# Four edits to a fused attention-and-routing kernel: who loads the first values, who clears the first tiles, how the weight sums are grouped, and the order of one block's products

## The chip, the cores and the metric

The kernel runs on one core of a Trainium2 chip. The metric is the device time of one execution in microseconds. Three runs of the kernel before took 889.56, 890.16 and 890.52 us; their median, 890.16 us, is the time that the change is measured against. The engines are named as in the profile: PE (matmuls) with its weight loads PEld, DVE (VectorE), ACT (ScalarE), POOL (GpSimd) and SP (SyncE, which here only issues DMAs).

## The reference, cut to what matters

```python
# attention: batch 4, heads 4, seq 1088, head_dim 32, r = 8; S1 and S2 arrive as float64
a = einsum('rd,bhsd->bhsr', S1, x); b = einsum('rd,bhsd->bhsr', S2, x)
phi(x) = outer(a, b) per row                      # 64 features
kv  = sum over s of phi(k) v^T ;  z = sum over s of phi(k)
out = phi(q) kv / (phi(q) z + 1e-6)               # -> x: (4352, 128)
# routing: 8 rounds of row and column normalisation of exp(x @ w_gate) -> P (4352 x 8)
# mixture: for each of 8 experts e
h = maximum(x @ w1[e], 0); out += P[:, e:e+1] * (h @ w2[e])   # w1: 128 x 1024, w2: 1024 x 128
```

The sum over `s` in `kv` and `z` runs over all keys of a batch, so the order in which keys lie in a tile is free as long as the values lie in the same order.

## The kernel before, in words

The kernel has three stretches on PE, one after the other without a break.

**Start (0 to about 21 us).** The loads of batch 0 are issued by SP in this order: S1 (L104; S2 goes by ACT's queue), the keys (`load_k`, L171), the first 8 of 34 rows of the queries (L178), the values (`load_v`, L180 to L189: four quarters of 128 KB at L183 and two short tails at L187), the other queries, then the first weights and batch 1. DVE turns S1 and S2 from float64 into float32 (`f64_to_f32`, L34 to L47), transposes them (`st`, L222) and spreads them over the heads (`wd`, L223). `transpose_k` (L266) then transposes the keys into `kT` in two halves (L269) and a rest (L271); `transpose_q` (L264) does the queries. PE multiplies `kT` by `wd` (L280), ACT copies the result to `ab` (L283), DVE forms the products of features `kp` (L295), and PE sums them against the values (L310, 36 matmuls in nine steps of four; the first four steps use the first half of `kp`). `kvz` (L326), the fractions (L369) and the division (L380 to L387) give `xT`, the input of the experts, and the first expert matmuls (L734) follow. POOL clears several tiles at the start (L113 to L165) and forms the repeated projections `wq` (L230, L231) from `st`. In each of these DVE, ACT and PE run in the order written in the code; POOL and SP are ordered by a scheduler. Every DMA uses one of eight completion semaphores in turn, so an issue also waits until the transfer eight issues before it has landed.

**Unweighted blocks (about 21 to 190 us).** Expert 0, and expert 1 for a part of the rows, in blocks of the hidden units (`steps`, L803). For each block PE computes four pieces `h[0..3]` (L734, relu by ACT at L736), DVE forms the sums `t13` (c = 4: `ts[0]` and `ts[1]` together), then `ts[2]` and `ts[3]` (L749), and PE makes seven products (`seven`, L769 to L784, issued by `into` at L796). Two products on different halves of the array run side by side; `p7` runs alone. `LAG` of 8 puts a block's products behind the pieces of the blocks after it, except at the very end, where no blocks follow. When an accumulator is complete, `part_of_seven` copies it out. In between, the rest of attention and the routing rounds are fitted in.

**Weighted stage (from 190 us).** 60 items (group of rows, expert), each in two halves `s = 0` and `s = 1` of eight steps. `firsts` (L1058) makes seven products per half into two PSUM pairs `pa` and `pc` (L1074), ACT copies some of them out (L1154, L1158, L1161), DVE adds them into `h` (L1084) and forms `ts` (L1131, L1134 to L1136). `seconds` (L1196) of the half before is interleaved step by step (L1224). In the first group, experts 1 to 7 come for the first time ("fresh"): their `w1` is loaded raw (L896) and POOL forms four sums of its parts (`sum_first`, L914: forms 4, 5, 6, 7 at L917 to L920), which are also stored for later groups (L923). `aside` (L1099), called after the third product of a half, hands POOL its work: the weighted inputs of the item after next (`weigh`, L1004), their difference (`sum_x` part 0, L1012), and in `s = 0` all four sums of the next fresh item. A `gate` (L1097) is a one-element copy by ACT into the target, which keeps POOL from starting before that point.

Of the kernel before, what the change touches and what calls it, by code (L numbers as in the profile page):

```python
# [10 lines left out]
F32 = mybir.dt.float32  # L11
U32 = mybir.dt.uint32
Act = mybir.ActivationFunctionType
Alu = mybir.AluOpType
# [4 lines left out]
def f64_to_f32(nc, pool, raw, shape):  # L19


    p, n = shape
    low, high = raw[:, 0::2], raw[:, 1::2]

    def u32(name):
        return pool.tile([p, n], U32, name=name)

    def f32(name):
        return pool.tile([p, n], F32, name=name)

    mant, bits, top, expo, rest = (u32(x) for x in ("mant", "bits", "top", "expo", "rest"))
    out, inside, over = f32("s12"), f32("inside"), bits.bitcast(F32)
    shift_right, shift_left = Alu.logical_shift_right, Alu.logical_shift_left
    nc.vector.tensor_scalar(bits, high, 3, 0x3F800000, op0=shift_left, op1=Alu.bitwise_and)  # L34
    nc.vector.tensor_scalar(mant, high, 3, 0x3FFFFFF8, op0=shift_left, op1=Alu.bitwise_and)
    nc.vector.tensor_scalar(rest, low, 0x1FFFFFFF, None, op0=Alu.bitwise_and)

    nc.vector.scalar_tensor_tensor(top, high, 0xC0000000, bits, op0=Alu.bitwise_and, op1=Alu.bitwise_or)
    nc.vector.scalar_tensor_tensor(mant, low, 29, mant, op0=shift_right, op1=Alu.bitwise_or)
    nc.vector.tensor_scalar(expo, high, 20, 0x7FF, op0=shift_right, op1=Alu.bitwise_and)  # L40
    nc.vector.scalar_tensor_tensor(out, rest, 2.0 ** -52, top.bitcast(F32), op0=Alu.mult, op1=Alu.mult)
    nc.vector.scalar_tensor_tensor(mant, high, 0xC0000000, mant, op0=Alu.bitwise_and, op1=Alu.bitwise_or)

    nc.vector.tensor_scalar(over, expo, 1150.5, 3e38, op0=Alu.is_ge, op1=Alu.mult)
    nc.vector.tensor_tensor(out, out, mant.bitcast(F32), op=Alu.add)
    nc.vector.scalar_tensor_tensor(inside, expo, 896.5, over, op0=Alu.is_ge, op1=Alu.add)
    nc.vector.tensor_tensor(out, out, inside, op=Alu.mult)  # L47
    return out


@with_exitstack
def kernel(
# [12 lines left out]
    nc = tc.nc  # L65
    P = nc.NUM_PARTITIONS
    B, H, S, D = q.shape
    R = S1.shape[0]
# [4 lines left out]
    SA = S // 32  # L73
    NT = S // P
# [5 lines left out]
    H2 = DM // 2  # L80

    consts = ctx.enter_context(tc.tile_pool(name="consts", bufs=1))
# [18 lines left out]
    words = mybir.dt.size(S1.dtype) // 4  # L101
# [32 lines left out]
    qT, kT = (wk.tile([P, 4 * W9], F32, name=n, bufs=1) for n in ("qT", "kT"))  # L134
# [14 lines left out]
    kvs = []  # L149
    for i in range(2):  # L150
        kvs.append(consts.tile([P, 2, 2, D + 1], F32, name=f"kvs{i}"))
        nc.gpsimd.memset(kvs[i], 0.0)

    eps = consts.tile([P, 3, H], F32, name="eps")
    nc.gpsimd.memset(eps, 1e-6 / P)

    v_slots = []
    for i in range(2):
        t = wk.tile([P, H + 1, NT + 1, D], F32, name=f"v{i}", bufs=1)
        nc.vector.memset(t[:, H], 1.0)  # L160
        nc.gpsimd.memset(t[H2:P, 0:H, NT], 0.0)
        v_slots.append(t)

    ab = wk.tile([P, 2, NT + 1, H * R], F32, name="ab", bufs=1)
    nc.gpsimd.memset(ab[H2:P, :, NT], 0.0)  # L165

    loaded, pools = {}, []

# [5 lines left out]
    def load_q(b, lo=0, hi=SA):  # L174
# [2 lines left out]
        x = q[b].rearrange("h (s a) d -> (h s) a d", a=SA)  # L177
        nc.sync.dma_start(out=loaded["q", b][:, lo:hi], in_=x[:, lo:hi])  # L178

    def load_v(b):  # L180
        vx, o = v_slots[b % 2], v[b].offset
        for c in range(4):
            nc.sync.dma_start(  # L183
                out=vx[c::4, 0:H, 0:NT, :].rearrange("p h t d -> p h (t d)"),
                in_=AP(tensor=v.tensor, offset=o + NT * D * c, ap=[[SA * D, 32], [S * D, H], [1, NT * D]]))
        for c in range(2):
            nc.sync.dma_start(  # L187
                out=vx[32 * c:32 * (c + 1), 0:H, NT, :],
                in_=AP(tensor=v.tensor, offset=o + (4 * NT + c) * D, ap=[[SA * D, 32], [S * D, H], [1, D]]))  # L189
# [24 lines left out]
    wd = consts.tile([P, 2, H, R], F32, name="wd")  # L214
# [2 lines left out]

    def projections():
        flat = raw.rearrange("p n d -> p (n d)")
        s12 = f64_to_f32(nc, consts, flat, (P, 2 * D)) if words == 2 else flat.bitcast(F32)  # L220
        st = consts.tile([P, 2, 32], F32, name="st")
        nc.vector.transpose(out=st.rearrange("p n r -> p (n r)"), in_=s12)  # L222
        nc.vector.tensor_tensor(wd, st[:, :, 0:R].unsqueeze(2).to_broadcast([P, 2, H, R]),  # L223
                                own.unsqueeze(1).unsqueeze(3).to_broadcast([P, 2, H, R]), op=Alu.mult)
        return st

# [15 lines left out]
    nothing = consts.tile([P, 1], F32, name="nothing")  # L242
# [23 lines left out]
    def transpose_k(b, parts=((0, NT),)):  # L266
        kx = loaded["k", b]
        for lo, hi in parts:
            nc.vector.transpose(out=kT[:, 0:NT * P].rearrange("p (t s c) -> p c t s", c=4, s=32)[:, :, lo:hi],  # L269
                                in_=kx[:, 0:4 * NT, :].rearrange("p (c t) d -> p c t d", c=4)[:, :, lo:hi])  # L270
        nc.vector.transpose(out=kT[:, NT * P:S], in_=kx[:, 4 * NT:SA, :].rearrange("p a d -> p (a d)"))  # L271

# [347 lines left out]
    loaded_w, sums, parts, done = {}, {}, {}, {}  # L620
# [91 lines left out]
    blocks = [(j, q) for j in range(len(items)) for q in range(FO // 2)]  # L712
# [56 lines left out]
    def seven(k):  # L769

        j, q = blocks[k]
        _, w2, ws = loaded_w[j]
        h, ts, _ = hs[k]
        lo, hi = slice(0, H2), slice(H2, DM)
        p1 = (w2[:, 2 * q, lo], h[0], 0, 0)
        p6 = (ws[:, 1, q], ts[2], 0, 1)
        p2 = (w2[:, 2 * q + 1, lo], h[2], 1, 0)
        p4 = (w2[:, 2 * q + 1, hi], ts[3], 1, 1)
        p3 = (ws[:, 3, q], h[3], 2, 0)
        p5 = (ws[:, 0, q], ts[0], 2, 1)  # L780
        p7 = (ws[:, 2, q], ts[1], 3, k % 2)
        if k % 2 == 0:
            return [p1, p6], [p2, p4], [p3, p5], [p7]
        return [p6, p1], [p4, p2], [p5, p3], [p7]  # L784
# [77 lines left out]
    fresh = {*range(len(wgroups[0][2]))}  # L862
    late = []
    forms, form_stores, weights, sources = {}, {}, {}, {}
    FORM = FO * H2 // 2

    PLACE = {f: n for n, f in enumerate((0, 4, 5, 7, 6, 2, 3, 1))}
# [43 lines left out]
            lo, hi = ((0, 2), (2, 3))[part_ - 2]  # L911
            in_turn(i, nc.sync.dma_start(out=ws[:, lo:hi], in_=f[:, 4 + lo:4 + hi]))

    def sum_first(i):  # L914
        g = nc.gpsimd
        w1 = {f: forms[i][0][:, n] for f, n in PLACE.items()}
        g.tensor_tensor(w1[4], w1[1], w1[3], op=Alu.add)  # L917
        g.tensor_tensor(w1[5], w1[4], w1[0], op=Alu.subtract)
        g.tensor_tensor(w1[6], w1[0], w1[1], op=Alu.subtract)
        g.tensor_tensor(w1[7], w1[2], w1[5], op=Alu.subtract)  # L920

    def store_first(i):
        nc.sync.dma_start(out=form_stores[witems[i][1]][0], in_=forms[i][0][:, 0:7])  # L923
# [116 lines left out]
    def weighted():  # L1040
# [12 lines left out]
        def rooms(t):  # L1053
            n = wgroups[witems[todo[t][0]][0]][1]
            base = hb[:, 4096 * (t % 2):4096 * (t % 2 + 1)]
            return [base[:, 2048 * a:2048 * a + 8 * n].rearrange("p (b n) -> p b n", b=4) for a in range(2)]

        def firsts(t):  # L1058

            i, s = todo[t]  # L1060
            g, e = witems[i]
            n = wgroups[g][1]
            a, c = pairs[::-1] if t % 2 and i else pairs
            w1, xf = forms[i][0], sources[i]
            h, ts = rooms(t)
            pa, pc = a[:, :, 0:n], c[:, :, 0:n]
            p1, p5, u2 = (copies[:, t % 2, m, 0:2 * n] for m in range(3))
# [28 lines left out]
            def gate(x, y):  # L1096
                nc.scalar.copy(x, y)  # L1097

            def aside(y):  # L1099


                if s == (i == 0) and i + 2 < len(witems):
                    weigh(i + 2, lambda x: gate(x, y))
                if 0 < i and i + 1 < len(witems) and s == (g > 0):
                    gate(sources[i + 1][:, 4, 0:1], y)
                    sum_x(i + 1, 0)
                if s == 0:
                    if 1 < i + 1 in fresh:
                        gate(forms[i + 1][0][:, PLACE[4], 0:1], y)
                        sum_first(i + 1)  # L1110
                    if 0 < i in fresh:
                        store_first(i)
                if g == 0:
                    pass
                elif chores and (s or not leisure):
                    chores.pop(0)[1]()
                else:
                    for _ in range(2 if g + 2 >= LAST else 1):
                        leave(nc.gpsimd)
# [279 lines left out]
        for t in range(len(todo) + 1):  # L1399
            if t < len(todo):  # L1400
                i, s = todo[t]
# [14 lines left out]
            s = seconds(t - 1) if t else iter(())  # L1416
# [9 lines left out]
    with tc.manual_schedule(engines={engines.DVE, engines.PE, engines.Activation}):  # L1426
        st = projections()
# [124 lines left out]
```

## Time and profile before

| | |
|---|---|
| median of three runs | 890.16 us |
| the profiled execution: its time / its span | 890.32 us / 888.5 us |
| granted PE clock, as a share of full speed | 1.00 |
| DVE, ACT, POOL busy | 765.5, 544.7, 274.9 us |
| mean DMA rate | 202 GB/s |

Times in the profile count from the start of the span, in microseconds. A row of the timeline has start, busy time, engine, line, operation, output and input tiles, shape and count; idle time of the engine before it and its releaser stand in square brackets. SPq rows are DMA issues, and landings come later. The chain of waits lists, in order of time, which work set the end: start, length, engine, tile, line, count. PE rows of fp32 matmuls count two passes per matmul, so x8 is four matmuls.

### The profile page before, as it was taken

The page shows a single profiled execution, that of the slowest core. Times are in us where ns is not written, and L with a number is a line of the kernel's source. Part 1 is how long each engine was busy: PE and PEld are TensorE (multiplying, and loading weights), DVE is VectorE, ACT ScalarE, POOL GpSimd, SP SyncE. Part 2 cuts the span into 40 slices and gives each one's busy share as a digit, 9 for nine tenths or more (in the row PEclk, how much of TensorE's full clock was granted, in tenths as well). Part 3 has the DMA queues.
Part 4 walks back from the last instruction along what each step waited for, and adds up shares of the span by engine and source line. Part 5 has one row for each costly group of instructions (what it writes and reads, how often), then busy time and mean ns, then how long its engine had stood idle before and what let it go on. Part 6 is the DMA issues. An engine that isn't in the chain of part 4 may idle for free.

```text
span 888.5 us, 36437 instructions
## 1 busy us (share of the span) xinstructions
PE 881.3 (99%) x15308; PEld 651.0 (73%) x15308; DVE 765.5 (86%) x1339; ACT 544.7 (61%) x1086; POOL 274.9 (31%) x316
## 2 busy tenths in 40 slices
PE   8999999999999999999999999999999999999998
PEld 5788656867666777677777777777877887897886
DVE  8689689978898888888888888888899899889996
ACT  3455557646656666666666666666666666666664
POOL 3121125455552223323222322332232233333311
PEclk9999999999999999999999999999999999999999
DMA  7989399887786866477567667655774874774861
GB/s 231 294 268 276 83 219 250 135 243 229 226 256 180 236 204 197 132 220 214 160 174 214 197 170 210 197 170 162 236 232 130 265 236 135 226 245 130 249 198 31
DMA packets 146419, 179.10 MB, mean 202 GB/s; under 512 B 55984, under 2 KB 93568, under 8 KB 145872
## 3 DMA queue, kind: packets, MB, share of 16 engines
q1 hardware_dynamic: 138624, 166.67, 64.6%
q0 software_dynamic: 6528, 9.95, 5.6%
q8 instruction: 121, 1.98, 0.9%
q14 instruction: 42, 0.34, 0.1%
q10 hardware_dynamic: 1104, 0.15, 0.1%
HBM read 134.22 MB, written 25.99 MB: 180 GB/s over the span
## 4 chain that ended last, share of the span: by engine, by line
PE 97%; DVE 2%; DMA 0%; ACT 0%; issue 0%; DVEq 0%; ACTq 0%
PE pair L1074 39%; PE s L1224 38%; PE a L734 9%; PE s L796 7%; PE a L310 1%; PE a L439 1%; DVE kT L269 0%; PE a L280 0%; PE s L349 0%; DVE hb L749 0%; PE s L1240 0%; DMA raw<-in_S_dram 0%; DVE hb L1084 0%; PE a L473 0%; PE a L403 0%
## 5 line engine op out<-in xcount | busy, mean ns | idle before, releaser
L1074 PE MATMUL pair<-xf,w1x 64*64 64x256 f32 (+1 forms) x6736 | 500.1, 366 | 0.2
L1074 PEld LDWEIGHTS pair<-xf,w1x 64*64 64x64 f32 x6736 | 258.7, 133 | 92.0 <-DVE hb L1084 6.3
L1084 DVE TENSOR_TENSOR hb<-pair,copies 128x512 f32<-128x512 f32 (+1 forms) x354 | 233.7, 662 | 63.7 <-PE pair L1074 25.7
L1224 PE MATMUL s<-hb,w 64*64 64x256 f32 (+1 forms) x3824 | 285.1, 365 | 0.0
L1224 PE MATMUL s<-hb,ws 64*64 64x256 f32 (+1 forms) x2848 | 212.6, 365 | 0.0
L1087 ACT ACTIVATE hb<-hb 128x512 f32<-128x512 f32 (+1 forms) x238 | 144.4, 608 | 101.7 <-DVE hb L1084 96.3
L1224 PEld LDWEIGHTS s<-hb,w 64*64 64x64 f32 x3824 | 149.8, 133 | 47.9
L1004 POOL TENSOR_TENSOR xf<-xT,pb 128x512 f32<-128x512 f32 (+1 forms) x60 | 73.9, 1231 | 254.6 <-ACT xf L1097 198.6
L1012 POOL TENSOR_TENSOR xf<-xf 128x512 f32<-128x512 f32 (+1 forms) x59 | 72.9, 1235 | 216.7 <-ACT xf L1097 105.1
L1224 PEld LDWEIGHTS s<-hb,ws 64*64 64x64 f32 x2848 | 111.5, 133 | 35.9 <-issue 0.4
L734 PE MATMUL a<-xT,w 128*64 128x416 f32 (+3 forms) x512 | 122.5, 465 | 0.0
L1087 ACT ACTIVATE hb<-pair 128x512 f32<-128x512 f32 (+1 forms) x126 | 72.5, 576 | 44.3 <-PE pair L1074 44.1
L736 ACT ACTIVATE hb<-a 128x416 f32<-128x416 f32 (+3 forms) x128 | 59.5, 468 | 63.6 <-PE a L734 57.2
L1131 DVE SCALAR_TENSOR_TENSOR hb<-hb 128x512 f32<-128x512 f32 (+1 forms) x118 | 80.6, 683 | 15.9 <-ACT hb L1087 3.4
L1161 ACT COPY copies<-pair 128x512 f32<-128x512 f32 (+1 forms) x118 | 66.5, 563 | 30.8 <-PE pair L1074 30.8
L1158 ACT COPY copies<-pair 128x512 f32<-128x512 f32 (+1 forms) x118 | 66.5, 563 | 29.7 <-PE pair L1074 29.7
L1154 ACT COPY copies<-pair 128x512 f32<-128x512 f32 (+1 forms) x118 | 66.6, 564 | 26.4 <-PE pair L1074 26.4
L1134 DVE TENSOR_TENSOR hb<-hb 128x512 f32<-128x512 f32 (+1 forms) x118 | 79.4, 673 | 2.9
L1136 DVE TENSOR_TENSOR hb<-hb 128x512 f32<-128x512 f32 (+1 forms) x118 | 81.2, 688 | 0.0
L1135 DVE SCALAR_TENSOR_TENSOR hb<-hb 128x512 f32<-128x512 f32 (+1 forms) x118 | 80.6, 683 | 0.0
L796 PE MATMUL s<-hb,ws 128*64 128x416 f32 (+3 forms) x224 | 72.1, 475 | 0.0
L749 DVE TENSOR_TENSOR hb<-hb 128x416 f32<-128x416 f32 (+7 forms) x84 | 57.0, 681 | 15.2 <-ACT hb L736 12.4
(191 smaller groups left out, 688.2 us busy)
## 6 DMA issues: line engine op xcount, KB each, us to landing
w1x<-w1x SPq DMA_DIRECT2D x135, 256.0 KB, 4.2
w<-w2x SPq DMA_DIRECT2D x103, 256.0 KB, 3.9
ws<-w2x SPq DMA_DIRECT2D x51, 256.0 KB, 3.3
pb<-pT SPq DMA_DIRECT2D x35, 256.0 KB, 4.0
xf<-xf SPq DMA_DIRECT2D x70, 128.0 KB, 2.9
ws<-w2x SPq DMA_DIRECT2D x52, 128.0 KB, 4.0
w1x<-w1x SPq DMA_DIRECT2D x7, 896.0 KB, 5.6
w1x<-w1x SPq DMA_DIRECT2D x45, 128.0 KB, 3.8
```

Of the source, the lines that this page charges most:

```text
L734: nc.tensor.matmul(ph[sl], loaded_w[j][0][:, P * f + H2 * s:P * f + H2 * (s + 1)], xT[:, at + lo:at + hi], start=True, stop=True, tile_pos ...
L796: nc.tensor.matmul(sums[g][i][H2 * s:H2 * (s + 1)], w, x, start=c == 1, stop=c == per, tile_position=(0, H2 * s))
L1004: nc.gpsimd.tensor_tensor(xf[:, 0:2].rearrange("p b n -> p (b n)"), xT[:, lo:lo + 2 * n], weights.pop(i), op=Alu.mult)
L1012: nc.gpsimd.tensor_tensor(xf[:, 4:6], xf[:, 1:4:2], xf[:, 0:2], op=Alu.subtract)
L1074: nc.tensor.matmul(out[H2 * col:H2 * (col + 1), r], w1[rows, PLACE[form], o:o + H2], xf[rows, x], start=start, stop=stop, tile_position=(H ...
L1084: nc.vector.tensor_tensor(flat(out, n), x, flat(y, n), op=Alu.add)
L1087: nc.scalar.activation(out=x, in_=y, func=Act.Relu)
L1131: nc.vector.scalar_tensor_tensor(ts[:, 0], h[:, 3], 0.0, h[:, 0], op0=Alu.max, op1=Alu.subtract)
L1134: nc.vector.tensor_tensor(ts[:, 2], h[:, 1], ts[:, 0], op=Alu.subtract)
L1135: nc.vector.scalar_tensor_tensor(ts[:, 1], h[:, 3], 0.0, h[:, 1], op0=Alu.max, op1=Alu.subtract)
L1136: nc.vector.tensor_tensor(ts[:, 3], h[:, 2], ts[:, 2], op=Alu.subtract)
L1224: yield lambda rho=rho, rows=rows, c=c: nc.tensor.matmul(acc[g][rho][q][H2 * half:H2 * (half + 1), n * place:n * (place + 1)], w[rows], fl ...
```

## The change

- **Start, loads.** For batch 0 the quarters of the values are 32 neighbouring partitions instead of every fourth partition, and `transpose_k` writes `kT` of batch 0 in the matching order, in which each run of 32 outputs lies contiguously (before, every fourth element). Quarters 0 and 2 stay on SP; quarters 1 and 3 are issued by ACT, after a one-element copy that reads `rest` (L36), a value made from S1 and S2.
- **Start, engines.** Six clears (`kvs` twice, `eps`, the tails of the two value tiles, `ab`) move from POOL to DVE, ahead of the conversion of S1 and S2. The product `wd` (L223) moves from DVE to POOL, ahead of `wq`.
- **Fresh items.** `sum_first` is called in two parts: forms 4 and 6 in `s = 0`, forms 5 and 7 in `s = 1`, each behind its own gate. In the built program this touches the five asides of items 1 to 5, and adds one ACT copy of one element to each.
- **The last unweighted block** issues `[p5, p3], [p7, p1], [p6, p2], [p4]` instead of `[p6, p1], [p4, p2], [p5, p3], [p7]`; the copies of the finished accumulators change their order with it.

On PE nothing else differs in order or count. On SP the two quarters that it no longer issues are the only difference in order.

```diff
@@ f64_to_f32
-    return out
+    return out, rest.bitcast(F32)
@@ tiles cleared at the start
-        nc.gpsimd.memset(kvs[i], 0.0)
+        nc.vector.memset(kvs[i], 0.0)
-    nc.gpsimd.memset(eps, 1e-6 / P)
+    nc.vector.memset(eps, 1e-6 / P)
-        nc.gpsimd.memset(t[H2:P, 0:H, NT], 0.0)
+        nc.vector.memset(t[H2:P, 0:H, NT], 0.0)
-    nc.gpsimd.memset(ab[H2:P, :, NT], 0.0)
+    nc.vector.memset(ab[H2:P, :, NT], 0.0)
@@ load_v
+    def quarters_of_v(b, cs, queue):
+        vx, o = v_slots[b % 2], v[b].offset
+        for c in cs:
+            queue.dma_start(
+                out=vx[32 * c:32 * (c + 1), 0:H, 0:NT, :].rearrange("p h t d -> p h (t d)"),
+                in_=AP(tensor=v.tensor, offset=o + NT * D * c, ap=[[SA * D, 32], [S * D, H], [1, NT * D]]))
+
     def load_v(b):
         vx, o = v_slots[b % 2], v[b].offset
-        for c in range(4):
+        if not b:
+            quarters_of_v(0, (0, 2), nc.sync)
+        for c in range(4 if b else 0):
@@ projections
-        s12 = f64_to_f32(nc, consts, flat, (P, 2 * D)) if words == 2 else flat.bitcast(F32)
+        s12, gate = f64_to_f32(nc, consts, flat, (P, 2 * D)) if words == 2 else (flat.bitcast(F32), flat.bitcast(F32))
+        nc.scalar.copy(nothing, gate[:, 0:1])
+        quarters_of_v(0, (1, 3), nc.scalar)
-        nc.vector.tensor_tensor(wd, st[:, :, 0:R].unsqueeze(2).to_broadcast([P, 2, H, R]),
+        nc.gpsimd.tensor_tensor(wd, st[:, :, 0:R].unsqueeze(2).to_broadcast([P, 2, H, R]),
@@ transpose_k
-            nc.vector.transpose(out=kT[:, 0:NT * P].rearrange("p (t s c) -> p c t s", c=4, s=32)[:, :, lo:hi],
+            order = "p (t s c) -> p c t s" if b else "p (t c s) -> p c t s"
+            nc.vector.transpose(out=kT[:, 0:NT * P].rearrange(order, c=4, s=32)[:, :, lo:hi],
@@ seven
+        if k + 1 == len(blocks):
+            return [p5, p3], [p7, p1], [p6, p2], [p4]
@@ sum_first
-    def sum_first(i):
+    def sum_first(i, parts=(0, 1)):
...
-        g.tensor_tensor(w1[4], w1[1], w1[3], op=Alu.add)
-        g.tensor_tensor(w1[5], w1[4], w1[0], op=Alu.subtract)
-        g.tensor_tensor(w1[6], w1[0], w1[1], op=Alu.subtract)
-        g.tensor_tensor(w1[7], w1[2], w1[5], op=Alu.subtract)
+        if 0 in parts:
+            g.tensor_tensor(w1[4], w1[1], w1[3], op=Alu.add)
+            g.tensor_tensor(w1[6], w1[0], w1[1], op=Alu.subtract)
+        if 1 in parts:
+            g.tensor_tensor(w1[5], w1[4], w1[0], op=Alu.subtract)
+            g.tensor_tensor(w1[7], w1[2], w1[5], op=Alu.subtract)
@@ aside
-                if s == 0:
-                    if 1 < i + 1 in fresh:
-                        gate(forms[i + 1][0][:, PLACE[4], 0:1], y)
-                        sum_first(i + 1)
-                    if 0 < i in fresh:
-                        store_first(i)
+                if 1 < i + 1 in fresh:
+                    gate(forms[i + 1][0][:, PLACE[4 + s], 0:1], y)
+                    sum_first(i + 1, (s,))
+                if s == 0 and 0 < i in fresh:
+                    store_first(i)
```

## The prediction

> **What bounds the kernel now.** I read the page first, then the chain of waits, then the timeline of the three places that the edits touch, and last the groups and windows around them.
>
> ```profile
> span 888.5 us, 36437 instructions
> PE 881.3 (99%) x15308; PEld 651.0 (73%) x15308; DVE 765.5 (86%) x1339; ACT 544.7 (61%) x1086; POOL 274.9 (31%) x316
> ```
>
> PE is the bound, and no edit changes its work. What can be won are places where PE, although shown busy, stands behind another engine; the chain of waits names them. In the first 16 us:
>
> ```profile
> 5.21 0.26 DVE st L222
> 5.56 0.35 DVE wd L223
> 5.92 1.93 DVE kT L269 x2
> 7.91 0.68 PE a L280 x16
> 9.76 2.25 PE a L310 x72
> ```
>
> At the end of the unweighted blocks, where the 3.05 us of DVE's three sums lie on the chain:
>
> ```profile
> 184.98 1.03 DVE hb L749
> 186.04 1.01 DVE hb L749
> 187.07 1.01 DVE hb L749
> 188.13 2.31 PE s L796 x10
> 190.44 4.26 PE pair L1074 x72
> ```
>
> And in the first weighted group, once per item, a PE step of 0.66 us where the others take 0.43:
>
> ```profile
> 211.12 0.43 PE s L1224 x8
> 211.55 0.66 PE pair L1074 x8
> ...
> 223.89 0.66 PE pair L1074 x8
> 236.21 0.66 PE pair L1074 x8
> 248.54 0.66 PE pair L1074 x8
> 260.87 0.66 PE pair L1074 x8
> ```
>
> **Part 1, the fresh items.** The five long steps lie one item apart (236.21 - 223.89 = 12.32 us), for items 1 to 5, the ones whose `aside` carries `sum_first`. The timeline ahead of one of them shows why:
>
> ```profile
> 232.25 1.03 DVE L1134 TENSOR_TENSOR hb<-hb 128x512 f32<-128x512 f32 x1
> 232.81 1.06 POOL L918 TENSOR_TENSOR w1x<-w1x 128x256 f32<-128x256 f32 x1
> 233.21 1.22 DVE L1135 SCALAR_TENSOR_TENSOR hb<-hb 128x512 f32<-128x512 f32 x1
> 233.84 1.17 POOL L919 TENSOR_TENSOR w1x<-w1x 128x256 f32<-128x256 f32 x1
> 234.11 0.59 ACT L1161 COPY copies<-pair 128x512 f32<-128x512 f32 x1 [0.28 <-PE pair L1074]
> 234.34 1.21 DVE L1136 TENSOR_TENSOR hb<-hb 128x512 f32<-128x512 f32 x1
> 234.97 1.17 POOL L920 TENSOR_TENSOR w1x<-w1x 128x256 f32<-128x256 f32 x1
> 235.48 1.27 DVE L1084 TENSOR_TENSOR hb<-pair,copies 128x512 f32<-128x512 f32 x2
> ```
>
> While POOL forms sums, DVE's three `ts` instructions take 1.03, 1.22 and 1.21 us. In an item of the second group (window 293.0 to 305.1), which has no such sums, L1136 takes 0.68:
>
> ```profile
> L1136 DVE TENSOR_TENSOR hb<-hb 128x512 f32<-128x512 f32 x2 | 1.4, 684 | 0.0
> ```
>
> So DVE reaches the `h` sum (L1084) only at 235.48, straight from L1136, and PE waits for it. After the change POOL stops after two sums, at 232.81 + 1.06 = 233.9. L1134 stays at 1.03, L1135 is free from 233.9 and ends near 234.2, L1136 takes 0.68 and ends near 234.8. L1084 then starts when ACT's copy is out (234.11 + 0.59 = 234.70) and PE's product is done, about 235.0: 0.45 us earlier, where 0.23 is needed. The other two sums start behind the gate of `s = 1`, at about 234.9, and meet L1084, which has one input in PSUM: beside L920 two of them took 1.27, so 0.64 each, no longer than alone. By about 236.6 both sums are done, and DVE's `ts` work of that half begins only after its third L1084, about 237.4, so they don't meet. POOL has nothing else there. The added one-element copy delays ACT by about 0.2, five times, where ACT had 0.28 of idle time (the L1161 row); behind it is a relu that waits for L1084 anyway. The two later sums are wanted in the next item, 5 us on. Gain: 5 x (0.66 - 0.43) = **1.15**. Bounds: 0, if the moved sums hold DVE up in `s = 1` as much as they do now in `s = 0`; 1.4, if the step after the long one loses a lag of 0.05 too.
>
> **Part 2, the last block.** `p6` needs `ts[2]` (DVE done at 187.07), `p4` needs `ts[3]` (188.1). From 188.13 PE still makes `p4|p2`, `p5|p3` and `p7`, 2.31 us for three slots, about 0.7 each with some wait in the last, before the weighted stage starts at 190.44. But `p5`, `p3`, `p7` and `p1` need only the first sum, done at 186.04. In the new order they fill PE from the end of its backlog, about 187.0, to 188.4; `p6|p2` follows to 189.1, `p4` to 189.8. That is 0.65 earlier. The next work, L1074, needs more than PE:
>
> ```profile
> L1007 SPq DMA_DIRECT2D xf<-xf x2: 533/568/602, 184.4 to 185.0; - x2
> DMA to landing us min/median/max: 4.8/4.8/4.8
> ```
>
> These two transfers swap the halves of the first item's input; the second is issued at 185.0 and lands 4.8 later, at 189.85. It isn't moved, so L1074 can start at about 190.0, not at 189.8: what is late next is this transfer. The reordered copies are as many as before, and the accumulators that they empty are wanted only after 190.44 + 4.26 = 194.7. I take **0.35**, between nothing (the transfer, or POOL's sums for item 0 behind it, take all) and 0.65.
>
> **Part 3, the start.** `wd` is 0.35 us of DVE time ahead of `kT`, but the keys may have landed no earlier than 5.9, so I count nothing for it. The new write order counts:
>
> ```profile
> L269 DVE STREAM_TRANSPOSE kT<-kx 128x512 f32<-128x512 f32 x2 | 2.0, 1076 | 0.0
> L269 DVE STREAM_TRANSPOSE kT<-kx 128x1024 f32<-128x1024 f32 x2 | 4.2, 2096 | 0.0
> L264 DVE STREAM_TRANSPOSE qT<-qx 128x1088 f32<-128x1088 f32 x2 | 2.6, 1286 | 0.0
> L264 DVE STREAM_TRANSPOSE qT<-qx 128x256 f32<-128x256 f32 x2 | 0.8, 414 | 0.0
> ```
>
> Contiguous output costs (1286 - 414) / 832 = 1.05 ns per column and 0.15 us besides, so 512 columns take 0.68; every fourth element costs 2 ns (2096 - 1076 over 512). Each half is 0.39 shorter: PE's first L280 comes 0.39 earlier, its second nearly 0.8. L310 starts some 0.7 earlier, near 9.1, but its later steps need the second half of `kp`, which DVE delivers only 0.4 earlier, so its end and all behind it move by about 0.45. What has to keep up:
>
> ```profile
> L183 SPq DMA_DIRECT2D v<-in_v_dram x4: 604/608/679, 2.8 to 4.8; - x4
> DMA to landing us min/median/max: 3.2/3.3/3.7
> ...
> 3.20 0.47 DVE L34 TENSOR_SCALAR bits<-raw 128x64 uint32<-128x64 uint32 x1 [1.45 <-DMA raw<-in_S_dram]
> 5.54 0.29 POOL L230 TENSOR_TENSOR wq<-st,half 128x64 f32<-128x64 f32 x1 [1.47 <-DVE st L222]
> 15.09 1.31 DVE L264 STREAM_TRANSPOSE kT<-qx 128x1088 f32<-128x1088 f32 x1
> ...
> 6.00:7.00 1.00, 0.03 (x2) 0.03 (x2) 1.00 (x2) 0.00 (x0) 1.00 (x6) 1.00 0.79 234
> 13.00:14.00 1.00, 1.00 (x11) 0.54 (x8) 0.66 (x3) 0.00 (x0) 0.00 (x0) 1.00 0.98 336
> ```
>
> The six clears, 596 columns, lie in DVE's 1.45 us of waiting for S1; at about 1 ns a column and some start cost each they take an estimated 0.8, and without that cover all behind would be 0.8 later. `wd` on POOL takes about 0.3, like L230 of the same size, from 5.54, and is done by 5.9, ahead of the first `kT` half at 6.6; `wq`, 0.3 later, is wanted only behind L280 (7.8 by then). On SP two issues less (2 x 0.61) bring forward the tails, the rest of the queries and batch 1, the latter by about 0.8 since one issue still waits for the keys' landing. L264 of batch 1 at 15.09 then needs its data 0.45 earlier, and the DMA engines had room (0.79 busy from 6 to 7 us, against 0.98 from 13 to 14). ACT issues its quarters once `rest` exists, from about 3.9, 0.6 each, with nothing else to do before L280's result; 3.2 to 3.7 from issue to landing puts the last at about 8.2, ahead of 9.1. I take **0.45**; bounds 0 (keys or batch 1 land no earlier) and 0.8.
>
> Sum: 1.15 + 0.35 + 0.45 = 1.95 us. The profiled execution, 890.32 (its span and 1.82 around it), becomes 888.37; it stood 0.16 above the median, and against the median the sum is 890.16 - 1.95 = **888.2**.
>
> **The rivals.**
>
> *The sums only move their stall.* If two sums and the gate hold DVE up in `s = 1`, PE waits there: part 1 gives 0 and the time is 889.4. For it: DVE has next to no idle time in the rows above. Against: L1084 beside L920, unslowed.
>
> *The start is hidden.* If the keys, or batch 1's queries at 15.09, land no earlier, part 3 gives 0: 888.7. For it: from 13 us the DMA engines are full.
>
> *The values come late (slower).* Each quarter now lies in 32 neighbouring partitions, and two queues share the engines with the keys. The quarters of today were issued from 2.8 to 4.8 and landed within 2 us, about 6.3 to 8.3. If the placement halves their rate, that is 2 us more: L310 cannot start before 10.3, and what is queued behind, L264 at 15.09 above all, is 2 us late: 890.16 + 2.0 - 1.5 = 890.7; at a third of the rate 892.7. It decides from a landing later than 9.1. For it: a whole transfer goes to a quarter of the partitions. Against: two such transfers run side by side, and the engines had room. [...]
>
> *The new order isn't seen.* If the transfer, or POOL's sums behind it, keep PE as late as now, part 2 gives 0: 888.6.
>
> **How the numbers follow.** The forecast has 0.57, with a range of its own from 887.4 to 888.9; the upper bounds together give 890.16 - 2.85 = 887.3. The moved stall has 0.14, the hidden start 0.11, the unseen order 0.06, the late values 0.12. About 0.2%, 1.8 us, is what a measurement of this kernel can tell from no change, so the edges are 888.4 and 891.9. Of the forecast nearly three quarters, 0.42, lies below 888.4, and 0.07 of the hidden start and the unseen order: faster 0.49. Half of the late values goes beyond 891.9, and 0.03 is for something unseen: slower 0.09. The rest, 0.42, is no change. The range is 887.3 to 890.2: about 0.1 is left out above, a few hundredths below.
>
> **What would show it.** Right: the 0.66 us steps are gone and items 1 to 5 take 12.1 us; L1136 of `s = 0` near 0.68; `kT` halves at 0.68; L310 near 9.1; L1074 first follows L1007's landing by 0.1 to 0.2. Wrong: L1134 to L1136 long in `s = 1`, with a PE step over 0.5 there; L310 waiting for values; L264 of batch 1 still at 15.1.

## The result and the profile after

Eleven executions of the changed kernel have a median of 888.37 us (887.58 to 889.79), eleven of the kernel before beside them 890.6 (889.56 to 893.02). The ratio is 0.9970, 95% interval 0.9962 to 0.9979: 2.7 us faster by it, 1.9 to 3.4 (the two medians differ by 2.2). The profiled execution took 888.37, its span 886.6.

From the page of the changed kernel, its head and the busy times; PE makes the same 15308 matmul passes in a span 1.9 us shorter, with 0.8 less busy time and 1.1 less idle time:

```profile
span 886.6 us, 36445 instructions
PE 880.5 (99%) x15308; PEld 657.7 (74%) x15308; DVE 764.1 (86%) x1344; ACT 546.2 (62%) x1092; POOL 270.6 (31%) x311
```

The lines have moved: L269 is now L281, L280 L292, L310 L322, L349 L361, L796 L810, L1007 L1023, L1074 L1090, L1084 L1100, L1134 to L1136 L1149 to L1151, L1224 L1239, and POOL's sums are L932 (form 4), L933 (form 6), L935 (form 5) and L936 (form 7). The chain of waits (start, length, what), at the start, at the end of the unweighted blocks and at two of the places where the 0.66 us steps stood:

```profile
1.50 4.58 DMA kx<-in_k_dram
...
6.11 0.72 DVE kT L281
6.83 0.14 issue
6.96 1.19 PE a L292 x32
...
9.42 2.48 PE a L322 x72
...
187.88 1.75 PE s L810 x9
189.62 0.59 PE pair L1090 x8
190.21 0.03 issue
190.25 1.92 PE pair L1090 x25
...
211.15 0.43 PE pair L1090 x8
...
259.49 0.43 PE pair L1090 x8
```

At the start the two halves of `kT` now take 0.7 each, yet PE's first product starts at 6.96, as before (6.97): the keys are waited for until 6.08, and behind `kT` there are 0.14 us in which nothing is shown. `s L810` runs on without a wait for DVE's sums. Where 3 us of DVE stood there is now a first step of `pair L1090` of 0.59 instead of 0.43. The long steps of the items are gone.

To see where the time went, the matmul passes of both executions were numbered and the start times of the same passes compared. The first pass starts at 1.00; the cuts lie at pass 162 (second visit of L349), 1792 (11 us ahead of the weighted stage), 2016 (9 us into it) and 3136 (behind the last of the five long steps):

```
us from pass to pass   to 162   162-1792   1792-2016   2016-3136   3136-end   span
before                  10.94     166.80       20.97       61.86     626.97   888.54
after                   10.86     166.77       20.67       60.62     626.65   886.59
difference              -0.08      -0.03       -0.30       -1.24      -0.32    -1.95
```

The three parts of the change lie in the first, third and fourth column: 0.08 + 0.30 + 1.24 = 1.62. The last column, where nothing was edited, gave 0.32 more in this pair.

### The profile page after: what moved, and what is told of

It reads as the page before. It is cut to its first block, busy times and chain, and to the rows that moved or that the text cites. A ratio compares the mean times of both kernels' runs of the same rounds, so it can differ in the third digit from the quotient of the medians.

```text
span 886.6 us, 36445 instructions
## 1 busy us (share of the span) xinstructions
PE 880.5 (99%) x15308; PEld 657.7 (74%) x15308; DVE 764.1 (86%) x1344; ACT 546.2 (62%) x1092; POOL 270.6 (31%) x311
## 4 chain that ended last, share of the span: by engine, by line
PE 98%; DVE 1%; DMA 1%; ACT 0%; issue 0%; SPq 0%; DVEq 0%
PE pair L1090 39%; PE s L1239 38%; PE a L746 9%; PE s L810 7%; PE a L322 1%; PE a L451 1%; DMA kx<-in_k_dram 1%; PE a L292 0%; DVE kT L281 0%; PE s L1255 0%; PE s L361 0%; PE a L485 0%; PE a L415 0%; DVE ph L372 0%; DVE kT L275 0%; DVE hb L1100 0%
## 5 line engine op out<-in xcount | busy, mean ns | idle before, releaser
L1090 PE MATMUL pair<-xf,w1x 64*64 64x256 f32 (+1 forms) x6736 | 502.0, 365 | 0.1
L1090 PEld LDWEIGHTS pair<-xf,w1x 64*64 64x64 f32 x6736 | 261.9, 133 | 87.7 <-DVE hb L1100 4.1
L1100 DVE TENSOR_TENSOR hb<-pair,copies 128x512 f32<-128x512 f32 (+1 forms) x354 | 234.1, 662 | 65.0 <-ACT xf L1113 24.7
L1239 PE MATMUL s<-hb,w 64*64 64x256 f32 (+1 forms) x3824 | 285.8, 365 | 0.0
L1239 PE MATMUL s<-hb,ws 64*64 64x256 f32 (+1 forms) x2848 | 213.7, 365 | 0.1
L1239 PEld LDWEIGHTS s<-hb,w 64*64 64x64 f32 x3824 | 150.6, 133 | 46.6
L1020 POOL TENSOR_TENSOR xf<-xT,pb 128x512 f32<-128x512 f32 (+1 forms) x60 | 73.9, 1231 | 248.0 <-ACT xf L1113 204.0
L1239 PEld LDWEIGHTS s<-hb,ws 64*64 64x64 f32 x2848 | 112.5, 133 | 35.0 <-issue 0.5
L1146 DVE SCALAR_TENSOR_TENSOR hb<-hb 128x512 f32<-128x512 f32 (+1 forms) x118 | 80.1, 679 | 13.9 <-ACT hb L1103 1.8
L1149 DVE TENSOR_TENSOR hb<-hb 128x512 f32<-128x512 f32 (+1 forms) x118 | 79.2, 672 | 3.0 <-DVE xf L1030 0.2
L1150 DVE SCALAR_TENSOR_TENSOR hb<-hb 128x512 f32<-128x512 f32 (+1 forms) x118 | 80.6, 683 | 0.0
L1151 DVE TENSOR_TENSOR hb<-hb 128x512 f32<-128x512 f32 (+1 forms) x118 | 78.5, 665 | 0.0
L810 PE MATMUL s<-hb,ws 128*64 128x416 f32 (+3 forms) x224 | 71.5, 475 | 0.0
```

Of the source, the lines that this page charges most:

```text
L810: nc.tensor.matmul(sums[g][i][H2 * s:H2 * (s + 1)], w, x, start=c == 1, stop=c == per, tile_position=(0, H2 * s))
L1020: nc.gpsimd.tensor_tensor(xf[:, 0:2].rearrange("p b n -> p (b n)"), xT[:, lo:lo + 2 * n], weights.pop(i), op=Alu.mult)
L1090: nc.tensor.matmul(out[H2 * col:H2 * (col + 1), r], w1[rows, PLACE[form], o:o + H2], xf[rows, x], start=start, stop=stop, tile_position=(H ...
L1100: nc.vector.tensor_tensor(flat(out, n), x, flat(y, n), op=Alu.add)
L1146: nc.vector.scalar_tensor_tensor(ts[:, 0], h[:, 3], 0.0, h[:, 0], op0=Alu.max, op1=Alu.subtract)
L1149: nc.vector.tensor_tensor(ts[:, 2], h[:, 1], ts[:, 0], op=Alu.subtract)
```

## The experiments

### The parts one by one

`e1_sums`: the kernel before with this alone:

```diff
-                if s == 0:
-                    if 1 < i + 1 in fresh:
-                        gate(forms[i + 1][0][:, PLACE[4], 0:1], y)
-                        sum_first(i + 1)
+                if 1 < i + 1 in fresh:
+                    gate(forms[i + 1][0][:, PLACE[4 + s], 0:1], y)
+                    sum_first(i + 1, (s,))
```

> The kernel before with the four sums of w1 in two pairs and nothing else. Theory (the change's gain is mainly this one: five steps of 0.66 us become 0.43): items 1 to 5 take about 12.08 us each instead of 12.32, the time is 1.1 to 1.25 below before's. Rival (the shift of 0.245 an item seen between the two traces needs the earlier start of the weighted stage as well): less than 0.8 below.

`e2_order`: the kernel before with this alone:

```diff
+        if k + 1 == len(blocks):
+            return [p5, p3], [p7, p1], [p6, p2], [p4]
         if k % 2 == 0:
```

> The kernel before with the last unweighted block's products in the new order and nothing else. Theory: the first L1074 then waits for the landing of the second swap of xf, 0.30 to 0.35 us earlier than today; the time is 0.3 below before's. Rival (the new order only helped because all before it ran 0.1 earlier): 0.1 or less.

`e3_start`: the kernel before with all edits of the start (clears, `wd`, quarters of `v`, write order of `kT`) and neither of the other two. `e4_no_start`: the two above together, without the start; their diffs are those of the change.

> The kernel before with the edits of the start alone (quarters of v on two queues, the new write order of kT, wd on POOL, the clears on DVE). Theory (the keys land 0.28 later and the first product waits 0.14 behind kT): first L280 not earlier than 6.9, L734 at 15.15, the time 0.1 below before's, at most 0.2. Rival (the start gives its predicted 0.45 and something behind it gave 0.35 back in the profiled run alone): 0.4 to 0.5 below, with the keys' wait over at 5.8.

> The whole change without its start. Theory: the parts add up, 1.2 + 0.3 = 1.5 below before's, so 0.1 to 0.2 behind the whole change's gain. Rival (the start is worth its 0.45): 0.5 or more behind it.

Ratios to the kernel before on the same chip: e1 0.9991 (0.9980 to 1.0002), e2 0.9994 (0.9984 to 1.0004), e3 1.0005 (0.9994 to 1.0016), e4 0.9983 (0.9970 to 0.9996). Single parts can't be told from no change by their times; e4, 1.5 us faster, fits 1.2 + 0.3. The start alone (e3) lies between 0.5 us faster and 1.4 slower, and e4's interval overlaps that of the whole change, so the times price the start neither way. The stretches of their profiles say more:

```
us from pass to pass   to 162   162-1792   1792-2016   2016-3136   3136-end   span
e1_sums                 10.96     166.97       22.08       60.63     626.86   888.49
e2_order                10.95     166.87       20.19       62.04     627.79   888.83
e3_start                10.44     166.79       21.18       61.87     629.31   890.59
e4_no_start             11.14     166.80       20.49       60.63     626.57   886.62
```

The fresh items take 60.63 wherever the sums are split, and 61.9 to 62.0 elsewhere, so the theory holds for e1 in its place; but e1 gave 1.1 of it back ahead of the items (22.08). In e2 the stretch with the new order is 0.78 shorter than before, more than the 0.30 to 0.35 expected. In e3 the first product stands at 6.54, so the rival was right there: that execution has the whole gain of 0.45 to 0.5, 0.16 of it because its `kT` began at 5.68 instead of 5.84. It then lost 2.3 in the last column. Of that, 1.5 lie in one place, where the chain of waits of e3 has

```profile
709.54 0.38 PE pair L1086 x8
709.92 1.52 issue
711.44 0.61 PE s L1236 x8
```

with no releaser shown, 700 us behind anything that e3 edits (its L1086 and L1236 are L1090 and L1239 of the changed kernel). So one profile each doesn't price the start or the order: both depend on when transfers land.

### The same kernel again, and `wd` back on DVE

`after_again` is the changed kernel unedited.

> The changed kernel once more, for a second profile. Theory (the 0.28 us by which its keys landed later was scatter of that execution, not the change): the first L292 follows the keys' landing by 0.88, the sums stage L361 at its second visit (11.86) by 5.78, whatever the landing is, and the landing lies anywhere from 5.5 to 6.1, as in the five other profiles. Rival (the values' transfers hold the keys back): the landing is at 6.0 or later again.

`e7_wd_dve`:

```diff
-        nc.gpsimd.tensor_tensor(wd, st[:, :, 0:R].unsqueeze(2).to_broadcast([P, 2, H, R]),
+        nc.vector.tensor_tensor(wd, st[:, :, 0:R].unsqueeze(2).to_broadcast([P, 2, H, R]),
```

> The changed kernel with wd formed on DVE again. Theory (behind kT the first product waits 0.14 instead of 0.05 because it now waits for POOL as well): the first L292 follows the end of the first kT by 0.05, so 0.09 is gained where the keys land after 5.85, and lost where they land earlier. Rival (POOL's wd has no part in it): 0.14 again.

`after_again` has a ratio of 0.9974 (0.9962 to 0.9985), the first result once more. Its keys' wait ended at 6.24, so the rival stands: with the new start the keys are late again. The distances behind them held exactly (7.12 - 6.24 = 0.88; 12.02 - 6.24 = 5.78). For e7 (0.9965, 0.9952 to 0.9978) the chain of waits has

```profile
1.50 4.90 DMA kx<-in_k_dram
...
6.43 0.72 DVE kT L281
7.15 0.04 issue
7.19 1.28 PE a L292 x32
```

and so 0.04 of issue behind `kT` instead of 0.14, as expected. In every profile with `wd` on POOL the first product follows the end of the first `kT` by 0.146 to 0.148, in every one with `wd` on DVE by 0.054 or 0.055, although POOL's `wd` was done at 5.53 in the changed kernel, 1.3 us earlier. The view of L292 in the changed kernel, from 5 to 7.4 us, has an instruction of PE's queue that e7 lacks:

```profile
L292 PEldq EVENT_SEMAPHORE  x1: 51/51/51, 6.9 to 6.9; - x1
```

It waits for DVE's `kT`, runs from 6.857 to 6.908, and the first weight load, which waits for POOL's `wd`, follows at 6.934. All nine profiles with `wd` on POOL have it, the five others don't. So the 0.09 goes with the extra waiting instruction of a product that waits for two engines instead of one.

### What makes the keys late

Over all profiles (times in us; the keys' last packet and the end of their wait are from the DMA records):

```
                     keys: last packet  wait over   first kT  first L280/L292   pass 162
before                       5.46         5.80        5.84        6.97         11.94
e1_sums                      5.17         5.51        5.85        6.98         11.95
e2_order                     5.40         5.73        5.85        6.97         11.94
e4_no_start                  5.64         6.00        6.03        7.17         12.14
after                        5.51         6.08        6.11        6.96         11.86
e3_start                     5.23         5.66        5.68        6.54         11.44
after_again                  5.61         6.24        6.27        7.12         12.02
e9_swap_first                5.53         6.08        6.10        6.96         11.85
e10_all_in_s1                5.79         6.30        6.33        7.19         12.08
e11_weights_late             5.55         6.03        6.05        6.91         11.81
e12_sums_twice               5.67         6.28        6.31        7.17         12.06
e7_wd_dve                    5.79         6.40        6.43        7.19         12.10
e5_one_queue                 5.59         6.05        6.07        6.93         11.82
e8_old_place                 5.21         5.56        5.59        6.82         11.71
```

From the first `kT` to pass 162 it is 6.10 or 6.11 with the old start, 5.75 with the new one, 5.67 in e7. That is what the write order gains: 0.35, and 0.43 without the wait for POOL. But with the old start the keys' wait ends 0.33 to 0.36 after their last packet, with the new one 0.43 to 0.63 after it. The last packet is later too, by 0.14 on average (four profiles against the seven with the whole new start), in ranges that overlap. Two runs ask why.

`e5_one_queue`: all quarters by SP.

```diff
-            quarters_of_v(0, (0, 2), nc.sync)
+            quarters_of_v(0, (0, 1, 2, 3), nc.sync)
...
-        nc.scalar.copy(nothing, gate[:, 0:1])
-        quarters_of_v(0, (1, 3), nc.scalar)
```

> The changed kernel with all four quarters of v issued by SP, each still in 32 neighbouring partitions. In the four profiles with the start of before the keys' wait ends 0.33 to 0.36 after the keys' last packet, in the six with the new start 0.43 to 0.63 after it. Theory (ACT's two quarters, whose packets begin in just that stretch, delay the keys' completion): the lag is 0.33 to 0.38 again, the keys land near 5.75 and L322 starts 3.34 after that, near 9.1. Rival (SP's quarters delay it, by lying in fewer partitions): the lag stays at 0.45 or more. In either case the quarters must land by 9.1, or L322 waits for them.

`e8_old_place`: two queues, but the old place and the old write order.

```diff
-                out=vx[32 * c:32 * (c + 1), 0:H, 0:NT, :].rearrange("p h t d -> p h (t d)"),
+                out=vx[c::4, 0:H, 0:NT, :].rearrange("p h t d -> p h (t d)"),
...
-            order = "p (t s c) -> p c t s" if b else "p (t c s) -> p c t s"
+            order = "p (t s c) -> p c t s"
```

> The changed kernel with the values where they were (each quarter in every fourth partition) and kT written in the old order, on two queues as in the changed kernel. With the quarters in neighbouring partitions the keys' wait ended 0.43 to 0.63 after their last packet on two queues and 0.46 on one, against 0.33 to 0.36 in the four profiles with the old start. Theory (the place of the quarters makes the keys late): the lag is 0.33 to 0.38, the first kT begins at 5.6 to 5.9. Rival (something else of the new start, such as ACT's transfers or the faster start of DVE, does it): a lag of 0.43 or more and the first kT at 6.0 or later. Both: the halves of kT take 1.07 again and the sums stage L361 comes 6.1 to 6.2 behind the first kT instead of 5.75.

The view of the tile `v` in the changed kernel, from 1 to 9 us (duration of an issue in ns, first and last start, then issue to landing):

```profile
L183 SPq DMA_DIRECT2D v<-in_v_dram x2: 432/432/432, 2.8 to 3.3; - x2
L183 ACTq DMA_DIRECT2D v<-in_v_dram x2: 415/432/450, 3.7 to 4.1; - x2
...
DMA to landing us min/median/max: 4.3/4.3/4.4
```

The same view of e5:

```profile
L183 SPq DMA_DIRECT2D v<-in_v_dram x4: 432/432/432, 2.8 to 4.2; - x4
...
DMA to landing us min/median/max: 4.5/4.6/4.7
```

The same view of e8, and then its first `kT` in the timeline of DVE:

```profile
L183 SPq DMA_DIRECT2D v<-in_v_dram x2: 604/646/687, 2.8 to 3.6; - x2
...
DMA to landing us min/median/max: 3.3/3.4/3.5
```

```profile
5.59 2.02 DVE L281 STREAM_TRANSPOSE kT<-kx 128x512 f32<-128x512 f32 x2 [0.25 <-DMA kx<-in_k_dram]
```

With one queue and the new place the lag is 0.46 (the rival), with two queues and the old place 0.35 (the theory). So, one profile each, it is the place (with the shorter issue that comes with it), not the second queue. A quarter of 128 KB in 32 neighbouring partitions takes 4.3 (the changed kernel) or 4.6 us (e5) from issue to landing, one spread over all partitions 3.3 (before) or 3.4 (e8), medians all: about a third more, and which part of these times is fixed no run here shows. The keys, whose transfer ends while the quarters flow, pay for a part of it. With the old place, `kT` cost its 1.0 again, and pass 162 came 6.12 behind the first `kT`, as expected. In e5 the last quarter landed at 9.02 and the last tail, which only the last of the nine steps needs, at 9.37; the first L320 (L322 of the changed kernel) started at 9.38, 3.31 behind `kT` as elsewhere, so it waited for neither. Ratios: e5 0.9985 (0.9972 to 0.9997), e8 0.9974 (0.9964 to 0.9983); neither can be told from the changed kernel.

### What caps the new order

In the changed kernel the view of the tile `xf`, from 181 to 192 us, has the swap of the first item's halves and who waits for it:

```profile
L1023 SPq DMA_DIRECT2D xf<-xf x4: 533/562/597, 184.7 to 186.6; - x4
...
who waited for it (us, times):
...
  PEld pair L1090: 0.5, 1
...
DMA to landing us min/median/max: 4.9/4.9/4.9
```

Stretch 1792 to 2016, which holds this, took 20.97, 22.08 and 21.18 with the old order (before, e1, e3: mean 21.4), and 20.19, 20.49, 20.67, 20.10, 20.66, 21.59, 21.45, 21.35 and 20.04 with the new one (e2, e4, after, after_again, e10, e7, e5, e8, e12, none of which edits this place otherwise: mean 20.7). With the new order it follows the landing of the second swap, counted from pass 1792: 20.0 to 20.2 where that comes 10.9 to 11.3 later (e2, e12, after_again), 20.5 to 20.7 at 11.6 to 11.9 (e4, after, e10), 21.35 to 21.6 at 12.55 to 12.7 (e8, e5, e7). With the old order and a landing at 11.1 and 11.3 (before, e3) it took 21.0 and 21.2, so the order itself is worth about 1.0 where the swap lands early. In e7 (21.59) the chain of waits shows why:

```profile
179.71 6.22 DMA w1x<-in_moe_w_dram
...
185.94 5.65 DMA xf<-xf
...
191.64 0.43 PE pair L1090
```

There the swap isn't issued when its data is ready, but when an earlier load of `w1x` has landed. Where that is early, PE doesn't wait; this is the chain of `after_again` (20.10):

```profile
187.88 1.90 PE s L810 x10
189.79 1.22 PE pair L1090 x17
```

`e9_swap_first` issues the swap ahead of two loads of second forms:

```diff
-        for part_ in range(4):
+        for part_ in range(2):
             load_second(0, part_)
-        for i in range(2):
-            weigh(i, lambda x: None)
+        weigh(0, lambda x: None)
+        for part_ in range(2, 4):
+            load_second(0, part_)
+        weigh(1, lambda x: None)
```

> The changed kernel with the two transfers that swap the halves of item 0's input issued ahead of the last two loads of its second forms. Theory (part 2 is capped by these two transfers, which wait on SP for the landings of pb and w1x before they are issued, at 184.7 and 185.3): they are issued about 183.4 and 184.2 and land by 189.1, the first L1090 follows the last L810 with no wait, 0.3 to 0.4 earlier than in the changed kernel; the time is 0.3 to 0.4 below the changed kernel's. Rival (another work takes the gain: PE's backlog or the forms): the first L1090 moves by less than 0.1, or a later one waits for ws.

`e11_weights_late` also puts item 1's weights behind it:

```diff
-        for i in range(2):
-            load_weights(i)
+        load_weights(0)
         open_forms()
         load_raw(0)
+        weigh(0, lambda x: None)
+        load_weights(1)
         for part_ in range(4):
             load_second(0, part_)
-        for i in range(2):
-            weigh(i, lambda x: None)
+        weigh(1, lambda x: None)
```

> The changed kernel with the weights of item 1 and the second forms of item 0 loaded behind the swap of item 0's input. Theory (how much part 2 gives is set by the landing of the second swap, which on SP stands behind transfers of varying landing; between records 1792 and 2016 of PE the executions took 20.1 to 21.6 us, 20.1 where PE did not wait for it): both swaps are issued by 183.5 and land before 188.6, the first L1090 steps follow the last L810 with no wait, and the stretch takes 20.1; 0.3 to 0.6 less than the changed kernel on average. Rival (what is loaded later is wanted as early): the wait comes back behind ws, w2 or item 1's input and the stretch or the next item is longer by it.

e9 failed in its place: the view of `xf` from 183 to 186 us has

```profile
L1023 SPq DMA_DIRECT2D xf<-xf x2: 508/520/533, 183.8 to 185.3; - x2
...
DMA to landing us min/median/max: 6.2/6.6/7.0
```

Its second swap went out only at 185.3, when item 1's routing weights (`pb`) had landed, and took over 6 us; the stretch was 21.31. e11 did what it was to do: the swaps went out at 183.2 and 183.7, PE had no wait, the stretch took 20.04. But the rival was right as well. Item 1's own work on POOL came later, and the next stretch took 61.47 instead of 60.62. The timeline of e11 shows there an instruction of DVE that is long beside POOL's product L1020:

```profile
200.85 1.72 POOL L1020 TENSOR_TENSOR xf<-xT,pb 128x512 f32<-128x512 f32 x1
...
201.47 1.65 DVE L1149 TENSOR_TENSOR hb<-hb 128x512 f32<-128x512 f32 x1
```

Ratios: e9 0.9965 (0.9952 to 0.9978), e11 0.9974 (0.9964 to 0.9984). No version was found that beats the changed kernel by more than the intervals.

### Whom the sums hold up

The timeline of the changed kernel in the place that the prediction showed for before, `s = 0` of the same item and the beginning of `s = 1`:

```profile
231.36 1.04 DVE L1149 TENSOR_TENSOR hb<-hb 128x512 f32<-128x512 f32 x1
231.81 1.18 POOL L933 TENSOR_TENSOR w1x<-w1x 128x256 f32<-128x256 f32 x1
232.32 1.22 DVE L1150 SCALAR_TENSOR_TENSOR hb<-hb 128x512 f32<-128x512 f32 x1
233.46 0.68 DVE L1151 TENSOR_TENSOR hb<-hb 128x512 f32<-128x512 f32 x1
234.15 1.48 DVE L1100 TENSOR_TENSOR hb<-pair,copies 128x512 f32<-128x512 f32 x2
234.23 0.73 POOL L935 TENSOR_TENSOR w1x<-w1x 128x256 f32<-128x256 f32 x1 [1.25 <-ACT w1x L1113]
```

`e10_all_in_s1` puts all four sums behind the gate of `s = 1`; `e12_sums_twice` does so too and calls `sum_first` there twice in a row:

```diff
-                if 1 < i + 1 in fresh:
-                    gate(forms[i + 1][0][:, PLACE[4 + s], 0:1], y)
-                    sum_first(i + 1, (s,))
+                if s == 1 and 1 < i + 1 in fresh:
+                    gate(forms[i + 1][0][:, PLACE[4], 0:1], y)
+                    sum_first(i + 1)
```

> The changed kernel with all four sums behind the gate of s = 1. Theory (a step of 0.66 us comes whenever a sum of POOL lies beside the scalar_tensor_tensor or the last subtraction of hb on DVE): four sums take 3.9 us from the gate, reach those instructions of s = 1, and the 0.66 steps are back in s = 1: items of 12.2 to 12.32 us and 0.6 to 1.2 us above the changed kernel. Rival (the stall belongs to s = 0, where the second half of an item starts): items stay at 12.08.

> The changed kernel with all four sums behind the gate of s = 1, and each formed twice (the second time with the same result). Theory (what lengthens DVE's instructions is a sum beside one that reads and writes SBUF alone; with all four in s = 1 they ended at 238.3, before L1149 to L1151 at 238.6 to 240.4): eight sums reach L1149 to L1151 of s = 1, these take 1.0 to 1.2 instead of 0.68, the 0.66 step is back and items 1 to 5 take 12.2 to 12.7. Rival (only s = 0 is sensitive): items of 12.09.

e10: 0.9971 (0.9960 to 0.9982), and 60.62 for the items, 12.09 each. The theory's forecast failed. Its timeline shows why:

```profile
236.33 0.73 POOL L935 TENSOR_TENSOR w1x<-w1x 128x256 f32<-128x256 f32 x1
236.33 0.69 DVE L1100 TENSOR_TENSOR hb<-pair,copies 128x512 f32<-128x512 f32 x1 [0.17 <-PE pair L1090]
237.13 1.27 POOL L936 TENSOR_TENSOR w1x<-w1x 128x256 f32<-128x256 f32 x1
237.74 0.95 DVE L1030 TENSOR_TENSOR xf<-xf 128x256 f32<-128x256 f32 x1
238.61 0.68 DVE L1149 TENSOR_TENSOR hb<-hb 128x512 f32<-128x512 f32 x1
```

Beside L1100, which reads one input from PSUM, a sum takes 0.73, not 1.0 to 1.2, so four end at 238.4, ahead of L1149 at 238.6; the expected 3.9 us had been taken from sums beside `hb<-hb`. L1146, which starts together with the last sum, takes its usual 0.69; L1030 behind it is long (0.95). e12 (1.0094, 1.0077 to 1.0111) makes the sums last. Its timeline in `s = 1`:

```profile
242.24 1.21 DVE L1150 TENSOR_TENSOR hb<-hb 128x512 f32<-128x512 f32 x1
242.86 1.17 POOL L933 TENSOR_TENSOR w1x<-w1x 128x256 f32<-128x256 f32 x1
243.37 1.21 DVE L1151 SCALAR_TENSOR_TENSOR hb<-hb 128x512 f32<-128x512 f32 x1
```

L1150 to L1152, which are L1149 to L1151 of the changed kernel, now take 1.21 each in `s = 1`, so `s = 0` has nothing special. The two engines' starts alternate there, 1.13 or 1.14 apart on each, where DVE's are 0.60 apart without sums (e10 from 238.61). L1147, which starts 0.03 ahead of the sum beside it, keeps 0.69. The items took 14.1 and 16.3, more than expected, but that number prices something else. In its chain of waits PE waits for the repeated sums themselves, which the next item's first products need:

```profile
244.03 1.14 POOL w1x L935
...
245.22 1.03 PE pair L1090 x5
```

The slowing is shown in both halves; that the 0.66 step follows in `s = 1` could not be separated.

## Why the prediction came out

**Its time** was 888.2, the sum 1.95 against the profiled execution, and the profiled pair differs by 1.95. That agreement is partly luck: the three parts gave 1.62 where 1.95 was expected, and 0.32 came from the last 627 us, where no edit lies and where single executions differ by up to 2.7 (626.6 to 629.3). Beyond the profiled pair the base moved as well: the eleven executions before have 890.6, not 890.16, and 1.95 below that is 888.65.

**Part 1** (1.15) is right in place, mechanism and size: 1.24 over five items in the pair, 60.6 against 61.9 to 62.0 in all profiles but e11 (61.47) and e12, which burden POOL. L1149 to L1151 took 1.04, 1.22 and 0.68 (forecast: 1.03, shorter, 0.68); the two later sums took 0.73 each beside L1100, which stayed at 0.7. L1150 did not come free as early as forecast, but the 0.23 needed was there. The rival of the moved stall is out.

**Part 2** (0.35): 0.30 in the pair, with the cause that was named, the second swap (eight passes of L1090 ran before its landing at 190.20, the others followed it by 0.05, not by 0.1 to 0.2). What the prediction lacked is that this landing is no constant. Because its issue waits for landings of earlier loads, the stretch varies by 1.5 us between profiles, and the new order is worth 0.7 by the means above (three draws against nine that spread by 1.1 and 1.5, so a rough figure), from nothing in e7 to about 1.0 where the swap lands early, more than the 0.65 that was its bound. The pair's 0.30 is one draw of each, so its nearness to 0.35 is luck.

**Part 3** (0.45) is the term that was mis-sized: 0.08 in the pair, 0.12 on average (pass 162 at 11.99 in the four profiles with the old start, at 11.87 in the seven with the whole new one). The step that failed is the sentence in which the end of L310 and all behind it move by 0.45, with the keys taken to land as before. The halves of `kT` did shrink to 0.7 and the write order gave 0.43; 0.09 went into PE's second wait, and of the keys' later landing (5.76 to 6.10 on average) 0.23 show, since `wd` had held DVE until 5.84 anyway. 0.43 - 0.09 - 0.23 = 0.11. The edit that the prediction counted at nothing, `wd`, does matter where the keys are early: `kT` began at 5.68 in e3 and at 5.59 in e8, while with `wd` on DVE it never began before 5.84. Two of the prediction's signs for this part came out against it: the first L310 (L322) moved from 9.69 to 9.42, not to 9.1, and L264 of batch 1 stayed near 15.1, at 15.01.

**The rivals.** "The values come late" saw the right transfers, and the slower landing is real (1 us a quarter), but the halved rate that it reckoned with was the author's assumption, which no run shows (from issue to landing a quarter took a third more), and the price fell elsewhere: L322 starts 3.31 behind the first `kT` in all profiles with the new start and `wd` on POOL, so it never waited for values; the keys did. "The start is hidden" comes nearest to what the start did, through the keys. The six clears on DVE cost nothing that is seen: L34 starts at 3.18, before at 3.20. The shorter SP queue did not bring batch 1 forward by the forecast 0.8: its keys were issued at 8.55 instead of 8.56, because SP now waited 1.4 us for the landing of the first keys and 0.6 more for that of a quarter of the values (8.11).

## What to carry to other kernels

When a transfer is re-laid so that an engine reads or writes contiguously, price it at the other transfers in flight too: the one that pays may be the one ahead of it (here the keys, complete 0.43 to 0.63 us behind their last packet instead of 0.33 to 0.36). A term that hangs on the landing of a transfer whose issue waits for other landings is a spread, not a number (here 20.04 to 21.59 us for one stretch), and one profile gives one draw of it. Here POOL's sums were cheap beside a DVE instruction that reads PSUM (0.73 and no delay) and dear beside those on SBUF alone (up to 1.27, and DVE's own at 1.04 to 1.22 instead of 0.68), so choose the place of such work by what DVE does there.

## What the runs showed of the hardware

- The first product, waiting for DVE and POOL, started 0.147 us behind DVE, against 0.054 when it waited for DVE alone, in nine and five profiles, each to within 0.002, though POOL had been done for 0.7 to 1.45 us. With two engines PE has an extra waiting instruction of 0.051 there.
- 128 KB into 32 neighbouring partitions took 4.0 to 4.6 us from issue to landing (medians of e3, the changed kernel, `after_again` and e5) against 3.0 to 3.4 when spread (e1, before, e8), though its issue was shorter (0.36 to 0.46 against 0.60 to 0.69). The 544 KB transfer ahead of it completed 0.43 to 0.63 behind its own last packet (nine profiles) instead of 0.33 to 0.36 (five).
- A POOL sum of 128x256 takes 0.73 beside DVE's L1100 and up to 1.27 beside DVE instructions with two SBUF inputs, which go from 0.68 to between 1.04 and 1.22 (1.65 beside the 128x512 product); a DVE instruction that starts just ahead of or with the sum keeps 0.69 (L1146 in e10, L1147 in e12).
- PE stood for 1.52 us at 709.9 in one profile with no releaser. What it was stays open.
